# One level of Strassen's method in the second product of a channel mixing: seven block products in place of eight

## The chip, the cores and the metric

The kernel runs on one core of a Trainium2 chip. The metric is the device time of one execution in microseconds (us). The median of three runs is compared before and after the change.

## What is computed

Attention with a window of 64 over 4 sequences of 576 tokens, then a gated block that mixes along the tokens, then a token mixing, and last the channel mixing, which is what the change touches. Tokens of all sequences together: 2304. Width 512, hidden width of the channel mixing 1536.

```python
def _moe2_ref(x, w_tok1, w_tok2, w_ch1, w_ch2):
    xt = x.transpose(0, 2, 1)
    h = np.maximum(xt @ w_tok1, 0.0) @ w_tok2
    u = x + h.transpose(0, 2, 1)
    h2 = np.maximum(u @ w_ch1, 0.0) @ w_ch2     # u: 2304 x 512, w_ch1: 512 x 1536, w_ch2: 1536 x 512
    return (u + h2).astype(np.float32)
```

The weights come as 64-bit floats.

## The kernel before

Every operand of a matrix product is a pair of two fp32r tiles, a rounded part h and a rest l, and a product is three matmuls: h·h, h·l, l·h (`mm3`, L128). So a tile that is to be multiplied is first copied by ScalarE into h, and VectorE subtracts to get l. A weight is read from HBM as 64-bit words into `wraw`, and `load_wide` (L110) makes it fp32: one `Abs` on ScalarE (L123), four integer steps on VectorE (`to_f32`, L56 to L62), then the cast to h on ScalarE (L125) and the subtraction to l on VectorE (L126).

The activations stay in SBUF as `U`, 128 partitions x 4 x 2304. Up to L513 the order of every engine is written out by hand (attention and the gated block). Behind that the order is a planner's: it simulates the program and lets each engine take, among the instructions that are ready in its simulation, the one that comes first in the program. The order it finds is then fixed, and each engine works through its queue in that order on the chip. A pool that is opened where another one was closed gets its memory; its tiles wait for the last readers and writers of what lay there.

The stages behind L513, as the program has them:

- `wout(c)` (L544): output product of the gated block, five chunks of 512 tokens (the last one 256).
- `x2nat(b)` (L563), `tok1(b)` (L573), `tok2(b)` (L586): the token mixing of sequence b. 20 transposes, 28 matmuls of 512 columns, 48 matmuls of 288 columns. VectorE adds the result of `tok2` to `U` (L594).
- Loads of the channel weights between these: `load_c1(pl, ft)` for the 12 column blocks of `w_ch1`, `load_c2(pl, k)` for the 12 row blocks of `w_ch2`. All 24 blocks stay in SBUF as h and l.
- The channel mixing (L689 to L707): chunks of 512 tokens, four full ones and one of 256. `uin(c)` (L635) splits the chunk of `U`. `ch1(u, ft)` (L645) makes one of 12 hidden tiles: 12 matmuls into a bank of `psmm`, a ReLU on ScalarE to `g3h` (L653) and the rest `g3l` on VectorE (L654). `ch2` (L657) adds its product to the four output banks `acc`: 12 matmuls (L664). The planner has `uin(0)` and three `ch1` of the first chunk (L666, L670, L679) at hand while the token mixing still runs. Behind each chunk VectorE adds `acc` to `U` (L706) and SP stores it (L707).

Names that the steps below use: `psmm` 3 banks, `psA` 5 banks, `nat` (splits of the token mixing), `hp` (hidden tiles of the token mixing), `lw` (work space of the loads). All DMAs are issued by SP in order.

## Time and profile before

| | us |
|---|---|
| median of 3 runs | 674.54 |
| runs | 674.00 to 675.59 |
| profiled execution, span from the first to the last instruction | 675.1 |
| TensorE busy in it | 646.6 (96%) |
| VectorE busy | 358.1 (53%) |
| ScalarE busy | 247.1 (37%) |
| GpSimd busy | 21.7 (3%) |

The profiled execution has no time of its own beside its span; the span stands for it, 0.6 us above the median of the runs. A busy TensorE in this profile means that a matmul is in flight; matmuls overlap, so how dense they run is read from the distance between their starts.

### The profile page before, as it was taken

To read this page: it belongs to the slowest core of one execution; us is meant where nothing else is said; L and a number is where in the kernel's file an instruction comes from. 1 tells how busy PE (TensorE), PEld (TensorE's weight loads), DVE (VectorE), ACT (ScalarE), POOL (GpSimd) and SP (SyncE) were. 2 spreads that over 40 slices of the span, in tenths; PEclk is the share of its full clock that TensorE was granted. 3 is DMA by queue.
4 is the path that set the end of the run, shared out by engine and by line. 5 is a ranking of instruction groups with operands and counts; after the bars stand their busy time and mean duration, and the time that the engine had idled before them with its cause. 6 is when DMAs were issued, how large, how long until landed. Compare 5 with 4: busy or idle time off the path is not lost.

```text
span 675.1 us, 10865 instructions
## 1 busy us (share of the span) xinstructions
PE 646.6 (96%) x4346; PEld 551.8 (82%) x4346; DVE 358.1 (53%) x900; ACT 247.1 (37%) x654; POOL 21.7 (3%) x49
## 2 busy tenths in 40 slices
...
GB/s 319 234 121 88 143 164 149 96 105 84 71 145 29 3 108 130 65 1 0 11 146 94 94 124 157 0 63 0 1 1 62 1 0 22 42 1 1 62 1 32
DMA packets 27954, 50.18 MB, mean 74 GB/s; under 512 B 2432, under 2 KB 12544, under 8 KB 27904
## 3 DMA queue, kind: packets, MB, share of 16 engines
...
q8 instruction: 34, 0.56, 0.4%
...
## 4 chain that ended last, share of the span: by engine, by line
PE 84%; DVE 7%; ACT 5%; DMA 3%; issue 1%; SPq 0%; POOL 0%; DVEq 0%; ACTq 0%
PE mm L136 51%; PE A L664 22%; PE A L136 4%; ACT pb L234 3%; PE sc L212 1%; PE xo L263 1%; PE A L570 1%; DVE pb L243 1%; ACT PT L252 1%; DMA raw<-in_wsT 1%; PE pt L251 1%; DMA msk<-in_mask 1%; DVE val L61 1%; DVE val L62 1%; PE mm L159 1%
## 5 line engine op out<-in xcount | busy, mean ns | idle before, releaser
L654 DVE SCALAR_TENSOR_TENSOR g3l<-mm,g3h 128x512 fp32r<-128x512 f32 (+1 forms) x60 | 38.2, 637 | 180.8 <-ACT g3h L653 180.6
L653 ACT ACTIVATE g3h<-mm 128x512 fp32r<-128x512 f32 (+1 forms) x60 | 33.4, 556 | 216.6 <-PE mm L136 216.5
L136 PE MATMUL mm<-uh,c1l 128*128 128x512 f32 (+1 forms) x240 | 89.0, 371 | 0.0
L136 PE MATMUL mm<-uh,c1h 128*128 128x512 f32 (+1 forms) x240 | 89.0, 371 | 0.0
L136 PE MATMUL mm<-ul,c1h 128*128 128x512 f32 (+1 forms) x240 | 88.9, 370 | 0.0
L664 PE MATMUL A<-g3h,c2l 128*128 128x512 f32 (+1 forms) x240 | 88.6, 371 | 0.0
L664 PE MATMUL A<-g3h,c2h 128*128 128x512 f32 (+1 forms) x240 | 87.5, 372 | 0.0
L664 PE MATMUL A<-g3l,c2h 128*128 128x512 f32 (+1 forms) x240 | 84.2, 372 | 0.0
L136 PEld LDWEIGHTS mm<-ul,c1h 128*128 128x128 f32 x240 | 45.2, 188 | 8.2
L664 PEld LDWEIGHTS A<-g3h,c2h 128*128 128x128 f32 x240 | 45.2, 188 | 8.2
L136 PEld LDWEIGHTS mm<-uh,c1h 128*128 128x128 f32 x240 | 45.3, 189 | 8.1
L136 PEld LDWEIGHTS mm<-uh,c1l 128*128 128x128 f32 x240 | 45.2, 188 | 8.2
L664 PEld LDWEIGHTS A<-g3h,c2l 128*128 128x128 f32 x240 | 45.2, 188 | 8.1
L664 PEld LDWEIGHTS A<-g3l,c2h 128*128 128x128 f32 x240 | 44.3, 188 | 8.3
L136 PE MATMUL mm<-ws_h,nh 128*128 128x288 f32 x160 | 47.5, 301 | 0.9 <-DVE tmp L354 0.9
L136 PE MATMUL mm<-ws_l,nh 128*128 128x288 f32 x160 | 46.5, 295 | 0.0
L234 ACT ACTIVATE pb<-pb,nm 128x128 f32<-128x128 f32 x96 | 37.2, 396 | 2.6 <-DVE nm L229 2.5
L136 PE MATMUL mm<-ws_h,nl 128*128 128x288 f32 x128 | 37.8, 295 | 0.0
L136 PE MATMUL mm<-xh,wi_h 128*128 128x384 f32 x96 | 32.6, 340 | 0.0
L136 PE MATMUL mm<-xh,wi_l 128*128 128x384 f32 x96 | 32.1, 334 | 0.0
L136 PE MATMUL mm<-xl,wi_h 128*128 128x384 f32 x96 | 32.1, 334 | 0.0
L136 PE MATMUL mm<-wi_h,xl 128*128 128x512 f32 x72 | 29.6, 411 | 2.1 <-DVE xl L272 2.0
...
## 6 DMA issues: line engine op xcount, KB each, us to landing
wraw<-in_w_c SPq DMA_DIRECT2D x24, 512.0 KB, 3.5
...
qq<-in_qT SPq DMA_DIRECT2D x18, 256.0 KB, 4.3
va<-in_v SPq DMA_DIRECT2D x18, 256.0 KB, 2.8
vb<-in_v SPq DMA_DIRECT2D x18, 256.0 KB, 3.3
U<-in_w_in SPq DMA_DIRECT2D x8, 512.0 KB, 6.9
outT<-U SPq DMA_DIRECT2D x16, 256.0 KB, 2.3
raw<-in_w_out SPq DMA_DIRECT2D x8, 256.0 KB, 2.9
```

The lines of the kernel that those rows point to most:

```text
L61: nc.vector.scalar_tensor_tensor(out=xi, in0=high, scalar=-0x40000000, in1=xi, op0=ALU.bitwise_and, op1=ALU.bitwise_or)
L62: nc.vector.scalar_tensor_tensor(out=xi, in0=low, scalar=29, in1=xi, op0=ALU.logical_shift_right, op1=ALU.bitwise_or)
L136: nc.tensor.matmul(o, a, c, start=(i == 0), stop=(i == n - 1))
L159: nc.tensor.matmul(ps.rearrange("p (a c) -> p a c", a=4), ident16, ident16.unsqueeze(1).to_broadcast([P, 4, 128]), start=True, stop=True)
L212: nc.tensor.matmul(scs[e][64 * q:64 * q + 64, j, :], qq[er, j, 64 * q:64 * q + 64], kk[er, j, step * q:step * q + 128], start=not on_pe, s ...
L234: nc.scalar.activation(out=pb[:, h, :], in_=scs[g][:, h - 4 * g, :] if mk is None else pb[:, h, :], func=AF.Exp, scale=SCALE, bias=nm[:, h ...
L243: nc.vector.tensor_tensor(out=half, in0=half, in1=rs.unsqueeze(2).to_broadcast([P, 4, 128]), op=ALU.mult)
L251: nc.tensor.transpose(pt[:, h, :], pb[:, 4 * g + h, :], ident)
L252: nc.scalar.copy(out=PT[:, 4 * g:4 * g + 4, :], in_=pt)
L653: nc.scalar.activation(out=gh, in_=ps, func=AF.Relu)
L654: nc.vector.scalar_tensor_tensor(out=gl, in0=ps, scalar=0.0, in1=f(gh), op0=ALU.max, op1=ALU.subtract)
L664: nc.tensor.matmul(acc[d], a, c, start=(ft == 0 and i == 0), stop=(ft == 11 and i == 2))
```

## The change

The second product of the channel mixing, `w_ch2`^T times the hidden activations, is cut in two by two blocks: the hidden width in halves of 768 (six tiles, `NJ` = 6), the output width in halves of 256, the tokens of a chunk in halves of 384 (`HW`). Seven block products take the place of eight, each of 6 x 2 x 3 matmuls of 384 columns. A chunk is now 768 tokens (`TW`), three chunks in all.

- `load_c2(j)` now makes, of rows j and j + 6 of `w_ch2`, the eight 256-column blocks that the method wants (four of them sums and differences by GpSimd), splits seven into h and l and writes them to a scratch tensor `scr` in HBM. Six calls: 0 to 2 during the token mixing, 3 to 5 in the first chunk.
- `ch1` makes 384-column halves and writes the ReLU as plain fp32 tiles `H` (30 buffers), by ScalarE alone. GpSimd makes the differences `e` and `b12` as the tiles come, and later, in place, those of `b11` and `b21` (`diff`).
- `product` reads the weights of a block product from `scr`, 512 KB at a time (`w`, 7 buffers), splits each hidden block into `oh` and `ol` (4 buffers each) by a ScalarE copy and a VectorE subtraction, and issues its 36 matmuls. `p1`, `u2`, `u3` hold partial results; VectorE (`vec`) and GpSimd add them to `U`, SP stores.
- The loads are in another order, `tok1(1)` now stands behind the closing of the pools of `wout`, and `uin(0)` stands behind the whole token mixing: its pool `up` opens where the work space of the loads (`lw3`, `xw`) was closed.

```diff
@@ -577,8 +577,8 @@
             ps = psA.tile([P, 512], F32, tag="A", name="A")
             mm3(ps, [(t1_h[:, s, jc], t1_l[:, s, jc], xn[b][s][0], xn[b][s][1]) for s in range(4)],
                 [(t1_h[:, 4, jc], xn[b][4]), (t1_l[:, 4, jc], xn[b][4])])
-            hh = hp.tile([P, 512], F32R, tag="hh", name="hh", bufs=2)
-            hl = hp.tile([P, 512], F32R, tag="hl", name="hl", bufs=2)
+            hh = hp.tile([P, 512], F32R, tag="hh", name="hh", bufs=hbufs)
+            hl = hp.tile([P, 512], F32R, tag="hl", name="hl", bufs=hbufs)
             nc.scalar.activation(out=hh, in_=ps, func=AF.Relu)
             nc.vector.scalar_tensor_tensor(out=hl, in0=ps, scalar=0.0, in1=f(hh), op0=ALU.max, op1=ALU.subtract)
             ht[b].append((hh, hl))
@@ -593,8 +593,11 @@
                 mm3(ps[:, :288], [(ht[b][j][0][:, dc], ht[b][j][1][:, dc], t2_h[:, j, cs], t2_l[:, j, cs]) for j in range(2)])
                 nc.vector.tensor_tensor(out=us, in0=ps[:, :288], in1=us, op=ALU.add)
 
-    c_stack = ExitStack()
-    c1, c2 = {}, {}
+    c_stack, x_stack = ExitStack(), ExitStack()
+    c1 = {}
+    hbufs = 2
+    HW, TW, NJ = 384, 768, 6
+    scr = tc.dram_tile([8, NJ // 2, P, 2, 2, 256], F32, name="scr")
 
     def load_c1(pl, ft):
 
@@ -602,110 +605,205 @@
         load_wide(lw, *[t.rearrange("p k c -> p (k c)") for t in c1[ft]],
                   w_c1[:, 128 * ft:128 * ft + 128].rearrange("(k p) c -> p k c", p=P), wmax=wmax)
 
-    def load_c2(pl, k):
-        c2[k] = [pl.tile([P, DM], F32R, name=f"c2{x}{k}") for x in "hl"]
-        load_wide(lw, *c2[k], w_c2[128 * k:128 * k + 128, :], wmax=wmax)
+    def fetch(dst, src):
+
+        raw = lw.tile([P, 2 * wmax], F32, tag="wraw", name="wraw", bufs=3).bitcast(I32)[:, :2 * DM]
+        nc.sync.dma_start(out=raw, in_=src.bitcast(I32))
+        r3 = raw.rearrange("p (n w) -> p n w", w=2)
+        nc.scalar.activation(out=dst, in_=f(r3[:, :, 1]), func=AF.Abs)
+        to_f32(dst, r3[:, :, 0], r3[:, :, 1])
+
+    def load_c2(j):
+
+        X = xw.tile([P, 8, 256], F32, tag="X", name="X", bufs=1)
+        for r, s in ((j, 0), (j + NJ, 2)):
+            fetch(X[:, s:s + 2, :].rearrange("p a c -> p (a c)"), w_c2[128 * r:128 * r + 128, :])
+        for o, a, b, op in ((4, 1, 3, ALU.add), (5, 4, 0, ALU.subtract), (6, 0, 1, ALU.subtract), (7, 2, 5, ALU.subtract)):
+            nc.gpsimd.tensor_tensor(out=X[:, o, :], in0=X[:, a, :], in1=X[:, b, :], op=op)
+        for s, n in ((0, 1), (2, 2), (4, 2), (6, 2)):
+            hl = xw.tile([P, 2, 2, 256], F32R, tag="hl", name="hl", bufs=3)[:, :n]
+            nc.scalar.copy(out=hl[:, :, 0, :], in_=X[:, s:s + n, :])
+            nc.vector.tensor_tensor(out=hl[:, :, 1, :], in0=X[:, s:s + n, :], in1=f(hl[:, :, 0, :]), op=ALU.subtract)
+            nc.sync.dma_start(out=scr[s:s + n, j // 2, :, j % 2].rearrange("s p h c -> p s h c"), in_=f(hl))
+
+    def xpool(stack, **kw):
+        return pool(f"xw{len(c1)}", stack=stack, bufs=1, **kw)
 
     wout(0)
     run_work(len(work))
     ws_stack.close()
     c1p = pool("c1p", "left", stack=c_stack, bufs=1)
-    hp = pool("hp", "left", stack=c_stack, bufs=1)
+    xw = xpool(x_stack, side="left")
+    hp = pool("hp", "left", stack=x_stack, bufs=1)
     wout(1)
     x2nat(0)
+    load_c1(c1p, 0)
     wout(2)
     tok1(0)
-    load_c1(c1p, 0)
+    load_c2(0)
     x2nat(1)
+    load_c1(c1p, 6)
     wout(3)
     tok2(0)
+    load_c2(1)
     load_c1(c1p, 1)
-    tok1(1)
     wout(4)
     x2nat(2)
-    load_c1(c1p, 2)
-    load_c1(c1p, 3)
+    load_c1(c1p, 7)
+    x_stack.close()
     g_stack.close()
 
 
-    p3 = pool("p3", "left", stack=c_stack, bufs=1)
+    c1q = pool("c1q", "left", stack=c_stack, bufs=1)
     wmax = DM
-    lw = pool("lw3", "left", stack=c_stack, bufs=1)
-
...
-    u0 = uin(0)
+    hbufs = 4
+    hp = pool("hp2", "right", stack=t_stack, bufs=1)
+    lw = pool("lw3", "left", stack=x_stack, bufs=1)
+    xw = xpool(x_stack, side="left")
+    tok1(1)
+    load_c2(2)
     tok2(1)
     tok1(2)
     x2nat(3)
-    g0 = [ch1(u0, ft) for ft in range(2)]
+    load_c1(c1q, 2)
+    load_c1(c1q, 8)
+    tok1(3)
     tok2(2)
-    load_c1(p3, 4)
-    load_c2(p3, 0)
-    tok1(3)
-    load_c1(p3, 5)
-    load_c2(p3, 1)
-    load_c2(p3, 2)
-    load_c1(p3, 6)
-    g0.append(ch1(u0, 2))
+    load_c1(c1q, 3)
+    load_c1(c1q, 9)
     tok2(3)
+    x_stack.close()
     t_stack.close()
     r_stack.close()
-    c2p = pool("c2p", "right", bufs=1)
-    load_c2(c2p, 3)
-    for k in range(4, 12):
-        load_c2(c2p, k)
-        if k < 9:
-            load_c1(c2p, k + 3)
-    chunks = range(-(-NTOK // CW))
-    for c in chunks:
-        u = uin(c) if c else u0
-        w = u[0].shape[-1]
-        acc = [psA.tile([P, 512], F32, tag="A", name="A")[:, :w] for _ in range(4)]
-        gq = [] if c else g0
-
-        late = 9 if c == chunks[-1] else 12
-        for ft in range(12):
-            while len(gq) < min(ft + 2, 12):
-                gq.append(ch1(u, len(gq)))
-            if ft < late:
-                ch2(acc, gq[ft], ft)
-        for d in range(4):
-            for ft in range(late, 12):
-                ch2(acc, gq[ft], ft, (d,))
-            ts_ = slice(CW * c, CW * c + w)
-            nc.vector.tensor_tensor(out=U[:, d, ts_], in0=acc[d], in1=U[:, d, ts_], op=ALU.add)
-            nc.sync.dma_start(out=outT[128 * d:128 * d + 128, ts_], in_=U[:, d, ts_])
+
+    up = pool("up", "left", stack=c_stack, bufs=1)
+    op_ = pool("op", "left", stack=c_stack, bufs=1)
+    Hp = pool("Hp", "right", stack=c_stack, bufs=1)
+    lw = pool("lw4", "left", stack=x_stack, bufs=1)
+    xw = xpool(x_stack, side="left")
+
+    def uin(c):
+        uh = up.tile([P, 4, TW], F32R, tag="uh", name="uh")
+        ul = up.tile([P, 4, TW], F32R, tag="ul", name="ul")
+        for h in range(2):
+            hs = slice(HW * h, HW * h + HW)
+            us = U[:, :, TW * c + HW * h:TW * c + HW * h + HW]
+            nc.scalar.copy(out=uh[:, :, hs], in_=us)
+            nc.vector.tensor_tensor(out=ul[:, :, hs], in0=us, in1=f(uh[:, :, hs]), op=ALU.subtract)
+        return uh, ul
+
+    def ch1(u, ft):
+
+        uh, ul = u
+        out = []
+        for h in range(2):
+            hs = slice(HW * h, HW * h + HW)
+            ps = psmm.tile([P, 512], F32, tag="mm", name="mm")[:, :HW]
+            mm3(ps, [(c1[ft][0][:, k, :], c1[ft][1][:, k, :], uh[:, k, hs], ul[:, k, hs]) for k in range(4)])
+            t = Hp.tile([P, HW], F32, tag="H", name="H", bufs=30)
+            nc.scalar.activation(out=t, in_=ps, func=AF.Relu)
+            out.append(t)
+        return out
+
+    def diff(out, a, b):
+        nc.gpsimd.tensor_tensor(out=out, in0=a, in1=b, op=ALU.subtract)
+        return out
+
+    def product(acc, slot, blk, first, last):
+
+        for jj in range(NJ // 2):
+            w = wr.tile([P, 2, 2, 256], F32R, tag="w", name="w", bufs=7)
+            nc.sync.dma_start(out=f(w), in_=scr[slot, jj])
+            for j in (2 * jj, 2 * jj + 1):
+                oh = op_.tile([P, HW], F32R, tag="oh", name="oh", bufs=4)
+                ol = op_.tile([P, HW], F32R, tag="ol", name="ol", bufs=4)
+                nc.scalar.copy(out=oh, in_=blk[j])
+                nc.vector.tensor_tensor(out=ol, in0=blk[j], in1=f(oh), op=ALU.subtract)
+                for d in range(2):
+                    dc = slice(128 * d, 128 * d + 128)
+                    todo = [(w[:, j % 2, 0, dc], oh), (w[:, j % 2, 1, dc], oh), (w[:, j % 2, 0, dc], ol)]
+                    for i, (a, m) in enumerate(todo):
+                        nc.tensor.matmul(acc[d], a, m, start=(first and j == 0 and i == 0),
+                                         stop=(last and j == NJ - 1 and i == 2), skip_group_check=True)
+
+    def banks():
+        return [psA.tile([P, 512], F32, tag="A", name="A")[:, :HW] for _ in range(2)]
+
+    u = None
+    for c in range(NTOK // TW):
+        t0 = TW * c
+        u = uin(c)
+        b11, b12, b21, b22, e = [], [], [], [], []
+        for j in range(NJ):
+            if c == 0 and j + 1 < NJ:
+                for ft in (j + 1, j + 1 + NJ):
+                    if ft not in c1:
+                        load_c1(c1q, ft)
+                if j < 3:
+                    load_c2(3 + j)
+            x, y = ch1(u, j)
+            b11.append(x)
+            b12.append(y)
+            x, y = ch1(u, j + NJ)
+            b21.append(x)
+            b22.append(y)
+            e.append(diff(Hp.tile([P, HW], F32, tag="H", name="H", bufs=30), b12[j], b11[j]))
+            diff(b12[j], b22[j], b12[j])
+        if c == 0:
+            x_stack.close()
+            wr = pool("wr", "left", stack=c_stack, bufs=1)
+        us = [[U[:, 2 * dh:2 * dh + 2, t0 + HW * h:t0 + HW * h + HW] for h in range(2)] for dh in range(2)]
+
+        def vec(dst, src, add, d, eng=nc.vector):
+            eng.tensor_tensor(out=dst, in0=src, in1=add, op=ALU.add)
+
+        def store(dh, h, d):
+            r = slice(256 * dh + 128 * d, 256 * dh + 128 * d + 128)
+            nc.sync.dma_start(out=outT[r, t0 + HW * h:t0 + HW * h + HW], in_=us[dh][h][:, d, :])
+
+        def tmp(tag):
+            return [wr.tile([P, HW], F32, tag=f"{tag}{d}", name=tag) for d in range(2)]
+
+        A = banks()
+        product(A, 0, b11, True, True)
+        p1 = tmp("p1")
+        for d in range(2):
+            nc.scalar.copy(out=p1[d], in_=A[d])
+            vec(us[1][0][:, d, :], us[1][0][:, d, :], p1[d], d, nc.gpsimd)
+        for j in range(NJ):
+            diff(b11[j], b22[j], e[j])
+        Bk = banks()
+        product(Bk, 5, b11, True, True)
+        u2 = tmp("u2")
+        for d in range(2):
+            vec(u2[d], Bk[d], p1[d], d)
+            vec(us[0][1][:, d, :], us[0][1][:, d, :], u2[d], d, nc.gpsimd)
+        product(A, 2, b21, False, True)
+        for d in range(2):
+            vec(us[0][0][:, d, :], A[d], us[0][0][:, d, :], d)
+            store(0, 0, d)
+        for j in range(NJ):
+            diff(b21[j], b21[j], b11[j])
+        product(Bk, 6, b12, False, True)
+        u3 = tmp("u3")
+        for d in range(2):
+            vec(u3[d], Bk[d], p1[d], d)
+            vec(us[1][1][:, d, :], us[1][1][:, d, :], u3[d], d, nc.gpsimd)
+        C = banks()
+        product(C, 4, e, True, True)
+        for d in range(2):
+            vec(us[1][1][:, d, :], C[d], us[1][1][:, d, :], d)
+            store(1, 1, d)
+        product(Bk, 3, b21, False, True)
+        for d in range(2):
+            vec(us[1][0][:, d, :], Bk[d], us[1][0][:, d, :], d)
+            store(1, 0, d)
+        product(C, 7, b22, False, True)
+        for d in range(2):
+            vec(us[0][1][:, d, :], C[d], us[0][1][:, d, :], d)
+            store(0, 1, d)
     c_stack.close()
+
 
 
 def kernel(**inputs):
```

## Rows read from the trace of the kernel before

**Rows 1.** The page: busy time by engine, transfer rate in 40 slices, chain by engine.

```profile
PE 646.6 (96%) x4346; PEld 551.8 (82%) x4346; DVE 358.1 (53%) x900; ACT 247.1 (37%) x654; POOL 21.7 (3%) x49
...
GB/s 319 234 121 88 143 164 149 96 105 84 71 145 29 3 108 130 65 1 0 11 146 94 94 124 157 0 63 0 1 1 62 1 0 22 42 1 1 62 1 32
...
PE 84%; DVE 7%; ACT 5%; DMA 3%; issue 1%; SPq 0%; POOL 0%; DVEq 0%; ACTq 0%
```

**Rows 2.** Busy time by stretch: us, then each engine (instructions), granted clock, DMA.

```profile
289.00:336.00 47.00, 47.00 (x268) 41.26 (x268) 15.77 (x29) 16.02 (x32) 0.00 (x0) 1.00 0.00 1
336.00:388.00 52.00, 52.00 (x303) 46.37 (x302) 42.75 (x79) 20.85 (x33) 0.00 (x0) 1.00 0.33 112
```

**Rows 3.** Chain of waits in order of time: start, us, what (x matmuls).

```profile
506.47 5.47 PE mm L136 x24
511.94 2.72 PE A L664 x12
...
525.99 2.80 PE A L664 x12
...
572.98 5.47 PE mm L136 x24
...
654.39 1.41 PE A L664 x12
```

**Rows 4.** Timeline of TensorE: start, us of one, line, tiles, shapes.

```profile
202.63 0.34 PE L136 MATMUL mm<-xl,wi_h 128*128 128x384 f32 x1
...
210.60 0.33 PE L136 MATMUL mm<-xh,wi_l 128*128 128x384 f32 x1
...
362.52 0.39 PE L664 MATMUL A<-g3h,c2h 128*128 128x512 f32 x1
...
364.01 0.39 PE L136 MATMUL A<-nl,t_h 128*128 128x512 f32 x1
```

**Rows 5.** Groups by line and shape: busy us, mean ns | idle before, releaser.

```profile
L61 DVE SCALAR_TENSOR_TENSOR wval<-wraw,wval 128x512 int32<-128x512 int32 x26 | 17.6, 684 | 0.1
...
L594 DVE TENSOR_TENSOR U<-mm,U 128x288 f32<-128x288 f32 x32 | 14.4, 454 | 22.0 <-PE mm L136 21.9
...
L58 DVE TENSOR_SCALAR wval<-wval 128x512 f32<-128x512 f32 x26 | 10.9, 422 | 3.0 <-ACT wval L123 2.5
...
L553 DVE TENSOR_TENSOR gl<-U,gh 128x512 fp32r<-128x512 f32 x16 | 10.4, 684 | 2.0 <-ACT gh L552 2.0
...
L552 ACT CAST gh<-U 128x512 fp32r<-128x512 f32 x16 | 9.2, 631 | 0.4 <-PE mm L136 0.3
...
L642 DVE TENSOR_TENSOR ul<-U,uh 128x2048 fp32r<-128x2048 f32 x4 | 9.1, 2286 | 2.2 <-ACT uh L641 2.2
...
L405 POOL TENSOR_TENSOR wi_l<-val,wi_h 128x512 fp32r<-128x512 f32 x4 | 5.1, 1280 | 9.1 <-ACT wi_h L403 9.1
...
L553 DVE TENSOR_TENSOR gl<-U,gh 128x256 fp32r<-128x256 f32 x4 | 1.7, 426 | 4.9 <-ACT gh L552 4.9
...
L552 ACT CAST gh<-U 128x256 fp32r<-128x256 f32 x4 | 1.6, 407 | 0.6 <-PE mm L136 0.5
```

**Rows 6.** Timeline of VectorE and GpSimd at two places in the hand-written part.

```profile
36.66 0.69 DVE L243 TENSOR_TENSOR pb<-pb,rs 128x512 f32<-128x512 f32 x1
37.33 1.27 POOL L405 TENSOR_TENSOR wi_l<-val,wi_h 128x512 fp32r<-128x512 f32 x1 [6.59 <-ACT wi_h L403]
37.67 1.48 DVE L243 TENSOR_TENSOR pb<-pb,rs 128x512 f32<-128x512 f32 x1
...
53.14 0.69 DVE L223 TENSOR_REDUCE mx<-sc 128x4 f32<-128x512 f32 x1
53.16 1.27 POOL L405 TENSOR_TENSOR wi_l<-val,wi_h 128x512 fp32r<-128x512 f32 x1 [2.46 <-ACT wi_h L403]
```

**Rows 7.** The page's DMA issues: engine, count, KB each, median us from issue to landing.

```profile
wraw<-in_w_c SPq DMA_DIRECT2D x24, 512.0 KB, 3.5
...
outT<-U SPq DMA_DIRECT2D x16, 256.0 KB, 2.3
```

38 lines of the change are left out of this document (7 added, 31 removed).

## The prediction

> **What bounds the kernel now.** I read the page first: TensorE is busy 96% of the span and makes 84% of the chain that ended last; VectorE is at 53%, GpSimd at 3% [rows 1]. A busy share says nothing of how dense the matmuls run, so the second view is the chain in order of time. From 506.47 to 572.98 it is TensorE alone: 24 matmuls of `ch1`, then 12 of `ch2` and 12 of `ch1` in turn, no wait between them [rows 3]. One such chunk is 12 x (12 + 12) = 288 matmuls, so its 66.51 us are 0.2309 us a matmul of 512 columns. Third, the stretches: TensorE has no idle time from 289 to 388 either, its granted clock is 1.00 (the 2.4 GHz level), while VectorE is busy 15.8 of 47 us in the first of them and 42.8 of 52 in the second [rows 2]. So the end is set by the number and the distance of matmuls, and VectorE is the engine next in line before 388. Fourth, the order: a `ch2` matmul at 362.52 stands between matmuls of `tok1` (the next one shown is at 364.01) [rows 4], though the program has them in separate calls. The queues are interleaved by the planner, and `ch1` and `ch2` of the first chunk fill holes of the token mixing.
>
> **The matmuls.** Before: four chunks of 66.51 us, and a last one with 256 columns, 12 matmuls of which take 1.41 us [rows 3], so 288 take 33.8 us. Together 299.9 us. After: a chunk has 24 halves of `ch1` with 12 matmuls (288) and 7 products with 36 (252); three chunks have 1620, all of 384 columns. The gated block has such matmuls: between the starts at 202.63 and 210.60 lie 46 steps [rows 4], 0.1733 us each. 1620 x 0.1733 = 280.7 us, a gain of 19.2 us. What may spoil it: `ch2` of 512 columns shows two speeds in one chunk, 2.72 and 2.80 us for 12 [rows 3], at the same clock, 6.7 ns a matmul apart. The rows of 384 show only one speed, so I take 0.1733; if all 1620 paid the 6.7 ns, 10.9 us of the gain would go. That is the other bound.
>
> The rows put 13 ns on a matmul of 384 columns beyond its 384 / 2.4 = 160 ns. The Trainium skill ("TensorE: Matmul & The Clock Gate", Back-to-back issue gap) has N / 2.4 + 2.5 ns; by that 1620 x 162.5 ns = 263.3 us against 1152 x 215.8 + 288 x 109.2 ns = 280.0 us, an estimate of 16.8 us gain. This case's rows are longer at every width, and the rows decide.
>
> **The splits, beside TensorE.** `ch1` loses the 60 subtractions of L654; each hidden block of a product costs a cast and a subtraction of 384 columns. The cast lies between 407 and 631 ns, the subtraction between 426 and 684 [rows 5]: 0.52 and 0.56 us. TensorE takes 6 x 0.1733 = 1.04 us for that block, so alone they are hidden; 126 of each add 65 us of ScalarE and 70 of VectorE to engines that were nearly idle there.
>
> **GpSimd beside VectorE.** A difference of 512 columns took GpSimd 1280 ns [rows 5]; 384 columns are 0.96 us. Per chunk 12 fall into `ch1` and 18 (12 differences, 6 additions to `U`) into the products. The trace shows what that does to VectorE: a two-input operation on SBUF (L243) takes 0.69 us alone; the one that started at 37.67, while GpSimd's subtraction ran from 37.33 to 38.60, took 1.48 and ended 0.55 us after GpSimd did. A reduction from PSUM (L223) beside GpSimd's next one kept its 0.69 [rows 6]. So `ol` (two SBUF inputs) and the differences exclude each other; VectorE's additions from PSUM don't. In the products of a chunk: 42 x 0.56 = 23.5 us of `ol`, 18 x 0.96 = 17.3 us of GpSimd, 3.4 us of the next `uin` (two of 0.75 x 2.286 us [rows 5]): 44.2 us against 42 x 1.04 = 43.7 us of matmuls. That just fits on average, but GpSimd's work is bunched. The differences of `b21` come ready one per block; a block then needs 0.56 + 0.96 = 1.52 us for TensorE's 1.04, 0.48 us lost per step. Four buffers of `ol` are three steps ahead, 3.1 us, less 1.1 us for cast and subtraction: 2.0 us of cover. Ten GpSimd operations in a row (two additions, six differences, two additions) cost 4.8 - 2.0 = 2.8 us. Below: 0, where the planner puts `ch1` of the next chunk into the hole, as it did at 362.52. Above: 5 us, two such rows without cover. One more wait is new there: on GpSimd the program puts two additions, which wait for the end of the first product and its copy `p1`, ahead of the differences of `b11`. Kept in that order, the second product starts late by a cast (0.52), three operations (2.9) and its first split (1.1), 4.5 us a chunk, which is within the upper bound. I take 2 us a chunk, 6 us in all, nearer to the lower end, since the planner is seen to fill holes; bounds 0 and 15.
>
> This is also where a page speaks against the change: the Trainium skill ("SBUF — State Buffer", SBUF: two separate sides) makes the port pair of VectorE and GpSimd an exclusive lock for a whole instruction. The trace agrees (1.48 us in place of 0.69).
>
> **The weights by way of HBM.** A product reads 3 x 512 KB per 6.24 us. Seven buffers are 7 x 2.08 = 14.6 us ahead; such a transfer lands 3.5 us after its issue [rows 7]. With seven loaded during `ch1`, the other 14 are 7.3 MB in 43.7 us, 168 GB/s; the first slice of the page moved 319 GB/s for 17 us [rows 1]. Hidden, 0 us. Without that cover see the second rival. Making the blocks costs VectorE, by call of `load_c2`: two conversions of 2 x 0.422 + 2 x 0.684 = 2.21 us, and splits of 0.43 + 3 x 0.684 = 2.48: 6.9 us, a `load_c1` 2.21 + 0.68 = 2.9 us [rows 5].
>
> **Up to 336.** Two `load_c2` go here, 13.8 us; VectorE has 31 us free from 289 to 336 [rows 2]. 0 us, at most 2.
>
> **End of the token mixing.** Behind 336 the changed program has three `tok1` (28 x 0.2267 = 6.35 us each), three `tok2` (48 of 288 columns; scaled from 0.1733, 6.35) and one `x2nat`: about 40 us of TensorE, and none of the `ch1` and `ch2` that filled it. VectorE has six ReLU rests (0.684), 24 additions (0.454), ten splits (0.68), one `load_c2` and four `load_c1`: 4.1 + 10.9 + 6.8 + 6.9 + 11.6 = 40.3 us in the same 40 us. And then `uin(0)`, whose memory comes free only behind the last of these loads: 1.7 us for its first half on VectorE, and about as much on ScalarE. Bounds: 0, if the loads run ahead; 9 us, if VectorE is only as dense as from 336 to 388, 42.75 of 52 [rows 2] (40.3 / 0.82 = 49). I take 4.
>
> **First chunk.** Until its sixth pair of `ch1`, 5 x 48 x 0.1733 = 41.6 us, three `load_c2` and four `load_c1` have to be through: 32.3 us of VectorE; GpSimd has 12 differences of 0.64 and ten of 0.96, 17.3 us. If all excluded each other, the last weights were 8 us late; if none, on time. I take 2: VectorE kept up at 42.75 of 52 without TensorE waiting [rows 2]. Later chunks need no loads, and their `uin` runs during products.
>
> **End.** The last block's store is of 192 KB, less than the 256 KB that land in 2.3 us [rows 7], more than the 128 KB of before: 0.2 us, at most 0.5.
>
> **Sum.** 675.1 - 19.2 + 6 + 4 + 2 + 0.2 = 668.1 us of span. The runs' median lies 0.6 us under this span, so 667.5 us. With all terms at the lower ends 655.5; its own range is 659 to 675.
>
> **Rivals.** (1) GpSimd locks VectorE out, slower. If every pair excludes and GpSimd's queue has the next operation ready each time, VectorE gets no turn within a bunch. From the start of the products to the end of the fourth, 24 `ol` (13.4), 17 to 18 GpSimd operations (17) and `uin` (3.4) need 34 us for 25 us of matmuls, less 2 of cover: 7 us a chunk, 21 in all; with 8 us in the first chunk and 4 before it 33 us: 688; half of it 678. It decides from 19.2 us of loss on. For: rows 6 and the sum of 44.2 against 43.7. Against: of the 18 operations only the six differences of `b11` have a reader in the next product, and they may begin before `ch1` is through. By the lock on the page named above it would come to the same time.
> (2) Weights behind stores, slower. SP works in order; a store waits for the end of a product and its addition. If weight loads are queued behind each of the four pairs of stores, a product begins 3.5 + 0.5 us late, four times a chunk, 48 us: 715. Against: 14.6 us of lead, and a planner that orders SP too.
> (3) The slow matmul speed at 384 columns: 667.5 + 10.9 = 678. Against: rows 4.
> (4) All holes filled: 655.5 to 659.
>
> **How the numbers follow.** Forecast 0.69, rival 1 0.14, rival 2 0.04, rival 3 0.05, rival 4 0.08. The range 657 to 680 leaves out half of rival 4, a good half of rival 1 and rival 2, some 0.17. A measurement of this kernel can tell about 0.2% (1.35 us) from no change: faster is under 673.2, slower over 675.9. Faster: 0.66 + 0.08 + 0.03 from the lower ends of rivals 1 and 3 = 0.77; same 0.04; slower 0.19.
>
> **What would show it.** Right: 384-column matmuls 0.173 us apart in `ch1` and in `product`; chunks of about 93.6 us (540 matmuls) plus 1 to 4; `ol` of 0.56 us alone and about 1.5 beside GpSimd; a hole of some us in TensorE before the first `ch1`; no wait for `w`. Wrong: a step of 0.18 us; TensorE waiting on `ol` in each product (rival 1), or on the DMA of `w` with a store in front of it on SP (rival 2); a hole before `ch1` well over 9 us, as the loads would then be the bound.

## The result and the profile after

| us | before | after |
|---|---|---|
| median of 4 runs each, measured together | 674.27 (673.01 to 675.59) | 668.79 (667.56 to 670.31) |
| ratio, 95% interval | | 0.9914 (0.9888 to 0.9940) |
| span of the profiled execution | 675.1 | 665.8 |

The change makes the kernel 5.5 us faster; 667.5 was forecast, 657 to 680 as the range. The profiled execution after is one of 667.56 us, 1.8 us above its span.

The page of after: busy time by engine, the groups of the new splits and differences, the transfers of the weights (columns as in [rows 1, 5, 7]).

```profile
PE 629.4 (95%) x4526; PEld 582.0 (87%) x4526; DVE 440.6 (66%) x995; ACT 317.1 (48%) x811; POOL 149.1 (22%) x163
...
L721 DVE TENSOR_TENSOR ol<-H,oh 128x384 fp32r<-128x384 f32 x126 | 95.4, 783 | 88.5 <-ACT oh L720 80.6
...
L709 POOL TENSOR_TENSOR H<-H 128x384 f32<-128x384 f32 x72 | 82.6, 1157 | 120.5 <-ACT H L704 80.3
...
w<-scr SPq DMA_DIRECT2D x63, 512.0 KB, 4.3
```

TensorE is 17 us less busy, VectorE 82 us more, GpSimd 127 us more [rows 1]. Where time went is read by stage. The first and last starts of some of TensorE's matmuls cut the end of the kernel in three: from the first matmul of `wout` to the first of `ch1` (token mixing), from there to the first of a product (first chunk), and from there to the end. First of before:

```profile
L136 PE MATMUL mm<-gh,wo_h x80: 280/389/487, 261.3 to 335.1; 128*128 128x512 f32 x64, 128*128 128x256 f32 x16
...
L664 PE MATMUL A<-g3l,c2h x240: 279/393/399, 363.8 to 671.1; 128*128 128x512 f32 x96, 128*128 128x256 f32 x24
```

Then of after (count, ns least/median/most, first and last start in us):

```profile
L136 PE MATMUL mm<-gh,wo_h x80: 278/389/485, 257.7 to 334.2; 128*128 128x512 f32 x64, 128*128 128x256 f32 x16
...
L136 PE MATMUL mm<-uh,c1h x288: 334/334/689, 369.4 to 617.3; 128*128 128x384 f32 x144
...
L726 PE MATMUL A<-oh,w x504: 334/334/346, 430.7 to 661.2; 128*128 128x384 f32 x168
...
L726 PE MATMUL A<-ol,w x252: 333/334/441, 431.0 to 661.5; 128*128 128x384 f32 x126
```

From the first matmul of `wout` to the last of all it is 671.1 - 261.3 = 409.8 us before and 661.5 - 257.7 = 403.8 after: 6.0 us less, which agrees with the medians. (`wout` begins 3.6 us earlier, in the part that the change doesn't touch; the kernels below begin it between 256.8 and 261.7. So stages are compared, not places.) The stretches of after, by engine:

```profile
369.40:430.70 61.30, 54.41 (x290) 51.99 (x290) 43.68 (x61) 26.96 (x53) 29.72 (x27) 0.94 0.58 203
430.70:524.40 93.70, 93.70 (x542) 93.70 (x541) 41.13 (x56) 36.22 (x70) 33.42 (x30) 1.00 0.47 157
524.40:618.00 93.60, 93.60 (x542) 93.60 (x541) 41.13 (x56) 36.23 (x70) 33.42 (x30) 1.00 0.42 135
618.00:662.00 44.00, 43.87 (x253) 43.36 (x251) 32.79 (x49) 20.70 (x41) 17.75 (x15) 1.00 0.60 195
```

Columns: stretch, us, then PE, PEld, DVE, ACT, POOL with instructions, granted clock, DMA share, GB/s. From the first product on TensorE has no hole: 540 matmuls in 93.6 us are 0.1733 us each. The loss is in the first line: 288 matmuls, 49.9 us at that pace, take 61.3. So the bill is 19.2 us gained on matmuls, 11.4 lost in the first chunk, and the remaining 1.8 lost in the token mixing (111.7 us, where before has 109.9: its 409.8 less the 299.9 of matmuls in its channel mixing).

What TensorE does in that hole, from its timeline (a group that waited has its wait in brackets):

```profile
410.79 0.34 PE L136 MATMUL mm<-uh,c1l 128*128 128x384 f32 x1
415.21 0.69 PE L136 MATMUL mm<-uh,c1h 128*128 128x384 f32 x1 [4.09 <-ACT c1h L125]
415.70 0.53 PE L136 MATMUL mm<-ul,c1h 128*128 128x384 f32 x1
...
421.13 0.33 PE L136 MATMUL mm<-uh,c1l 128*128 128x384 f32 x1
```

The stretch behind the longest wait, with the granted clock (0.51) as the third number from the end:

```profile
415.21:421.10 5.89, 5.84 (x17) 5.34 (x18) 5.86 (x10) 2.13 (x5) 1.39 (x2) 0.51 0.48 179
```

What TensorE waited for from 369 to 431 (us in total, times, longest):

```profile
PE mm L136 <- ACT c1h L125: 4.1, 1, 4.1
PE mm L136 <- ACT H L704: 1.8, 2, 1.4
PE mm L136 <- DVE c1l L126: 1.0, 1, 1.0
```

The larger part is for blocks of `w_ch1`, the rest for ScalarE's ReLU. By the starts, five waits between 394 and 417 are 7.9 us. Behind the longest one, 4.2 us by the starts, the matmuls stand 0.32 us apart and not 0.1733: the granted clock is at its lower level (1.2 GHz) from 415.21 to 421.1, 17 matmuls in 5.9 us for 2.9. One of the five waits, 0.4 us, lies in that stretch, so the clock costs some 2.6 us; the rest of the 11.4 is smaller delays.

Why the block is late, first from what SyncE's queue waited for (369 to 432):

```profile
SPq L611 <- PE mm L136: 10.2, 1, 10.2
```

and its issues in order:

```profile
369.55 7.21 SPq L611 DMA_DIRECT2D wraw<-in_w_c  x4
...
393.88 0.38 SPq L118 DMA_DIRECT2D wraw<-in_w_c  x1
```

The reads of the last three `load_c2` (L611) waited 10.2 us for a matmul of `tok2(3)` and began as it ended: the work space `lw4` and `xw` lies where the hidden tiles of the token mixing (`hp2`) lay. The first of the last four `load_c1` (L118) is issued 24 us later, behind all six of those reads. And then VectorE, by group and shape, with GpSimd behind it, in this stretch:

```profile
L626 DVE TENSOR_TENSOR hl<-X,hl 128x512 fp32r<-128x512 f32 x9 | 9.2, 1018 | 4.8 <-ACT hl L625 4.6
L61 DVE SCALAR_TENSOR_TENSOR X<-wraw,X 128x512 int32<-128x512 int32 x6 | 5.3, 892 | 0.1
L60 DVE TENSOR_SCALAR X<-X 128x512 int32<-128x512 int32 x6 | 4.2, 693 | 0.1
L62 DVE SCALAR_TENSOR_TENSOR X<-wraw,X 128x512 int32<-128x512 int32 x6 | 4.0, 681 | 0.0
...
L709 POOL TENSOR_TENSOR H<-H 128x384 f32<-128x384 f32 x15 | 19.2, 1291 | 14.6 <-ACT H L704 14.6
L622 POOL TENSOR_TENSOR X<-X 128x256 f32<-128x256 f32 x12 | 10.8, 907 | 38.1 <-DVE X L62 37.8
```

The split of 512 columns takes 1.02 us here for 0.68 in [rows 5], the shift of L60 0.69 for 0.42. So two causes offer themselves: loads that start late, and conversions that GpSimd makes longer. The experiments test them.

### The profile page after: what moved, and what is told of

It reads as the page before. It is cut to its first block, busy times and chain, and to the rows that moved or that the text cites. A ratio compares the mean times of both kernels' runs of the same rounds, so it can differ in the third digit from the quotient of the medians.

```text
span 665.8 us, 12069 instructions
## 1 busy us (share of the span) xinstructions
PE 629.4 (95%) x4526; PEld 582.0 (87%) x4526; DVE 440.6 (66%) x995; ACT 317.1 (48%) x811; POOL 149.1 (22%) x163
## 4 chain that ended last, share of the span: by engine, by line
PE 43%; DVE 3%; DMA 2%; POOL 1%; issue 1%; ACT 1%; DVEq 0%; POOLq 0%; ACTq 0%; SPq 0%
PE mm L136 21%; PE A L726 20%; PE A L136 2%; DMA wraw<-in_w_c 2%; POOL H L709 1%; DVE X L58 0%; DVE hl L626 0%; POOL X L622 0%; DVE X L61 0%; DVE wval L62 0%; DVE wval L61 0%; PE A L570 0%; DVE nl L295 0%; DVE wval L60 0%; DVE X L62 0%
## 5 line engine op out<-in xcount | busy, mean ns | idle before, releaser
L721 DVE TENSOR_TENSOR ol<-H,oh 128x384 fp32r<-128x384 f32 x126 | 95.4, 783 | 88.5 <-ACT oh L720 80.6
L726 PE MATMUL A<-oh,w 128*128 128x384 f32 x504 | 113.8, 334 | 0.0
L709 POOL TENSOR_TENSOR H<-H 128x384 f32<-128x384 f32 x72 | 82.6, 1157 | 120.5 <-ACT H L704 80.3
L136 PE MATMUL mm<-uh,c1h 128*128 128x384 f32 x288 | 97.4, 341 | 5.9 <-ACT c1h L125 4.1
L136 PE MATMUL mm<-uh,c1l 128*128 128x384 f32 x288 | 96.8, 338 | 1.0 <-DVE c1l L126 1.0
L136 PE MATMUL mm<-ul,c1h 128*128 128x384 f32 x288 | 96.9, 338 | 0.0
L720 ACT CAST oh<-H 128x384 fp32r<-128x384 f32 x126 | 64.2, 515 | 67.1 <-PE A L726 51.9
L726 PEld LDWEIGHTS A<-oh,w 128*128 128x128 f32 x504 | 89.7, 188 | 0.0
L726 PE MATMUL A<-ol,w 128*128 128x384 f32 x252 | 69.8, 334 | 0.0
L726 PEld LDWEIGHTS A<-ol,w 128*128 128x128 f32 x252 | 45.9, 188 | 0.2 <-DVE ol L721 0.2
L252 ACT COPY PT<-pt 128x512 f32<-128x512 f32 x36 | 19.7, 592 | 30.4 <-PE pt L251 30.4
```

The costliest lines, as they stand in the source:

```text
L136: nc.tensor.matmul(o, a, c, start=(i == 0), stop=(i == n - 1))
L252: nc.scalar.copy(out=PT[:, 4 * g:4 * g + 4, :], in_=pt)
L709: nc.gpsimd.tensor_tensor(out=out, in0=a, in1=b, op=ALU.subtract)
L720: nc.scalar.copy(out=oh, in_=blk[j])
L721: nc.vector.tensor_tensor(out=ol, in0=blk[j], in1=f(oh), op=ALU.subtract)
L726: nc.tensor.matmul(acc[d], a, m, start=(first and j == 0 and i == 0), stop=(last and j == NJ - 1 and i == 2), skip_group_check=True)
```

## The experiments

All medians are of 4 runs unless said; the kernel before ran beside them (medians 674.7 to 675.0). The stages are read as above, from first starts, and the last one ends with the last `oh` matmul. Each is read from one execution. After, e4 and e6 have the same program up to the products and differ there by 1.9 us (172.6 to 174.5), so smaller differences between sums of stages say little:

| kernel | median us | token mixing | first chunk | products | first two together |
|---|---|---|---|---|---|
| after | 668.79 | 111.7 | 61.3 | 230.5 | 173.0 |
| e1_c1_first | 668.75 | 111.7 | 60.3 | 233.2 | 172.0 |
| e2_no_sums | 662.63 | 111.9 | 56.2 | 230.5 | 168.1 |
| e3_room | 663.54 | 113.6 | 54.5 | 230.5 | 168.1 |
| e7_both | 664.62 | 115.9 | 51.8 | 230.5 | 167.7 |
| e8_vec_sums | 666.05 | 111.0 | 59.4 | 230.5 | 170.4 |
| e9_x2 | 665.27 | 113.8 | 55.4 | 230.6 | 169.2 |
| e12_c1f_vec_x2 | 665.15 | 118.9 | 49.9 | 230.5 | 168.8 |
| e13_room3_x | 660.69 | 113.9 | 50.9 | 230.5 | 164.8 |
| e14_order | 663.19 | 116.7 | 49.9 | 230.5 | 166.6 |
| e4_eight | 688.73 | 112.4 | 62.1 | 249.3 | 174.5 |
| e5_twice (10 runs) | 675.30 | 111.9 | 65.1 | 233.8 | 177.0 |
| e6_w2 | 689.49 | 111.4 | 61.2 | 249.5 | 172.6 |

**The hole: is it the order of the loads?** e1_c1_first puts the last four `load_c1` ahead.

```diff
-            if c == 0 and j + 1 < NJ:
-                for ft in (j + 1, j + 1 + NJ):
-                    if ft not in c1:
-                        load_c1(c1q, ft)
-                if j < 3:
-                    load_c2(3 + j)
+            if c == 0 and j < 3:
+                if j < 2:
+                    load_c1(c1q, 4 + j)
+                    load_c1(c1q, 10 + j)
+                load_c2(3 + j)
```

> The changed kernel lost about 11 us in TensorE between 390 and 431, in the first chunk. Here only the order of the loads in that chunk is changed: the four load_c1 come ahead of the second and third load_c2. Theory A, the order is at fault (the column blocks of w_ch1 stand behind three load_c2 in the queues): no TensorE wait for c1h or c1l any more, the hole goes and the time falls by 8 to 11 us against the changed kernel (668.8), to about 658 to 661. Theory B, the whole of the conversions starts too late (the memory of lw4 and xw is free only when the token mixing has ended, at 369.5) and takes some 50 us whatever the order: the hole moves from ch1 to the front of the first product, which waits for the first w; the time stays within 2 us of 668.8.

Measured 668.75, ratio to before 0.9916 (0.9887 to 0.9945): no change. What TensorE waited for from 368 to 429 in this kernel:

```profile
PE mm L136 <- ACT H L704: 3.8, 4, 2.7
PE A L726 <- DMA w<-scr: 3.2, 1, 3.2
```

No wait for a block of `w_ch1` is left; now the first product waits for its weights, which are read back only when the last `load_c2` is through, and 2.7 us more go in the products. The order alone only moves the hole.

**Is it where the loads start?** e3_room opens the pool of `oh` and `ol` behind the loads, so their work space moves down by 12 KB a partition, and halves the buffers of `hp2`, so that the raw reads don't lie on it any more and `xw` less.

```diff
-    hbufs = 4
+    hbufs = 2
-    op_ = pool("op", "left", stack=c_stack, bufs=1)
...
         if c == 0:
             x_stack.close()
+            op_ = pool("op", "left", stack=c_stack, bufs=1)
```

> Pools alone: op (oh and ol) is opened together with wr behind the loads, and hp2 has 2 buffers in place of 4, so that lw4 and the front of the last xw lie beside hp2 and not on it. The loads of the first chunk can then start when the work space of the loads before is free, about 352, not at 369.5. Theory B: the 11 us hole goes nearly whole, 657 to 661; the first product starts its splits only behind the loads, which may cost up to 2 us. Theory A: the order is as before, so ch1 still waits for its c1, by less: 662 to 666. Theory C: the conversions are as slow as before but earlier, so the same as theory B; only e2 tells these two apart.

Measured 663.54, ratio 0.9836 (0.9794 to 0.9878), 5.3 us better than after, less than this theory wanted.

```profile
L136 PE MATMUL mm<-uh,c1h x288: 334/334/522, 374.4 to 615.6; 128*128 128x384 f32 x144
...
L725 PE MATMUL A<-oh,w x504: 334/334/346, 428.9 to 659.4; 128*128 128x384 f32 x168
```

The first chunk takes 54.5 us instead of 61.3; the token mixing pays 1.9 of it back. Only the raw reads came earlier: the first conversion of the fourth `load_c2` still started at 374.6, as `X` kept waiting for the end of `tok2(3)`. The median lies in the range of theory A, but TensorE waits for no block of `w_ch1` in this chunk. Its one wait is for a ReLU, and the ReLU stood in ScalarE's queue behind the `Abs` of a `load_c1` (L123) whose read had not landed:

```profile
407.40 0.67 ACT L123 ACTIVATE wval<-wraw 128x512 f32<-128x512 f32 x1 [2.39 <-DMA wraw<-in_w_c]
407.98 0.47 ACT L703 ACTIVATE H<-mm 128x384 f32<-128x384 f32 x1
...
408.50 0.44 PE L136 MATMUL mm<-uh,c1h 128*128 128x384 f32 x1 [2.51 <-ACT H L703]
```

So a queue that loads and ReLUs share is a third thing that can hold TensorE up; no run tests it alone. e7_both adds e1's order to e3:

> The edits of e1 and e3 together. Theory B: as e3 or 1 to 2 us better, 656 to 660. Theory A: the order is what counts, so as e1. If the hole is gone, the rest of the sum holds: TensorE without a wait from 257 to the end, about 657 us.

Measured 664.62, ratio 0.9844 (0.9804 to 0.9884), above the 656 to 660 of theory B and not told apart from e3. The first chunk is down to 51.8, but the four `load_c1` now run on VectorE beside the token mixing, which takes 115.9.

**Is it GpSimd in VectorE's way?** e2_no_sums leaves the four sums of GpSimd out of the last three `load_c2`; other blocks are split and stored in their place, so only the sums are missing.

```diff
-        for o, a, b, op in ((4, 1, 3, ALU.add), ...):
+        for o, a, b, op in () if j > 2 else ((4, 1, 3, ALU.add), ...):
...
+            r = s % 4 if j > 2 else s
-            nc.scalar.copy(out=hl[:, :, 0, :], in_=X[:, s:s + n, :])
+            nc.scalar.copy(out=hl[:, :, 0, :], in_=X[:, r:r + n, :])
```

> The four sums on GpSimd are left out of the last three load_c2 (the unsummed blocks are split and stored in their place, so these weights are other numbers); the rest is the changed kernel. Theory C, GpSimd keeps VectorE out of its port during the conversions: VectorE's operations in the first chunk fall back to their lone durations but for the differences of H, and the hole of 11 us shrinks by 4 to 8 us, to about 661 to 665. Theory B (late start): the chain of a load_c2 loses only the time of the sums that are not hidden, the hole shrinks by 0 to 3 us, to about 666 to 669.

Measured 662.63, ratio 0.9817 (0.9787 to 0.9846): 6.2 us for twelve operations of 0.9 us. But this has two readings: VectorE's steps get shorter, or the chain within one `load_c2` (conversion, four sums, splits, then the next block in the same `X`) does. e8_vec_sums and e9_x2 try to tell them apart. In e8 VectorE makes those sums:

```diff
-            nc.gpsimd.tensor_tensor(out=X[:, o, :], ...
+            (nc.vector if j > 2 else nc.gpsimd).tensor_tensor(out=X[:, o, :], ...
```

> Nothing is left out: in the last three load_c2 the four sums of 256 columns are made by VectorE in place of GpSimd. Leaving them out gave 662.6. Theory C, VectorE is short of time in the first chunk, and GpSimd's exclusion makes its steps longer: the exclusion goes, but 12 x 0.43 = 5.2 us of VectorE come, so 666 to 669. Theory D, the chain of one load_c2 through its single X (conversion, four GpSimd steps of 1 us, splits, then the next block) is what is long: each chain gets 4 - 1.7 = 2.3 us shorter, three of them 6.9 us, so about as without the sums, 662 to 664.

Measured 666.05, ratio 0.9882 (0.9848 to 0.9915), in the range that theory C, VectorE's time, gave. One sum on VectorE (its row: count, ns least/median/most, starts):

```profile
L622 DVE TENSOR_TENSOR X<-X x12: 411/414/1122, 376.1 to 408.8; 128x256 f32<-128x256 f32 x12
```

The first chunk of e2, then of e8:

```profile
370.10:426.30 56.20, 52.91 (x290) 52.59 (x289) 39.92 (x61) 26.69 (x53) 19.98 (x15) 0.94 0.64 222
...
368.10:427.50 59.40, 54.03 (x291) 52.27 (x290) 44.90 (x73) 27.17 (x53) 18.92 (x15) 0.94 0.60 209
```

And what VectorE waited for in a `load_c2`, ScalarE's copy `hl`, in the first chunk of after, then of e8:

```profile
DVE hl L626 <- ACT hl L625: 4.9, 6, 2.3
...
DVE hl L626 <- ACT hl L625: 0.3, 1, 0.3
```

Without the sums VectorE is 3.8 us less busy than in after (39.92 for 43.68). In e8 it is 1.2 us busier than in after, and yet the chunk is 1.9 us shorter, as it waits 4.6 us less. So the time follows theory C, but the steps from engine to engine within a `load_c2` have a part in the 6.2 us; the two parts are not separated.

e9 is e3 with a second buffer for `X`, so that two blocks can be under way:

```diff
-        X = xw.tile([P, 8, 256], F32, tag="X", name="X", bufs=1)
+        X = xw.tile([P, 8, 256], F32, tag="X", name="X", bufs=2 if j > 2 else 1)
```

> As e3_room (pool op opened behind the loads, hidden tiles of the token mixing in two buffers), and X with two buffers in the last three load_c2, so that a block's conversion need not wait for the splits of the block before. Theory D (chain through the single X): 3 to 5 us under e3_room's 663.5, so 658 to 661. Theory C (VectorE is short of time, lengthened by GpSimd): as e3_room, 662 to 665.

Measured 665.27, ratio 0.9862 (0.9833 to 0.9890): no better than e3, and 0.3 above the range of theory C. So the single `X` by itself isn't what holds. VectorE waits 0.4 us for `hl` in the first chunk, where e3 has 4.1, but is busy 43.5 us for 40.2, and GpSimd 32.7 for 30.4: the wait has turned into longer operations, which fits two engines that exclude each other.

**Both causes together.** e12_c1f_vec_x2 is e7 with VectorE's sums and the second `X`:

> Nothing left out: e7_both (room, and the last four load_c1 ahead), with the sums of the last three load_c2 by VectorE and two buffers of X. If the first chunk is bound by VectorE's and GpSimd's time alone, the gains add: 664.6 - 2.7 = 662, and what remains is in the token mixing, which e7 slowed by 4.5 us between 360 and 370. If the chain through X was what held up the rest, 659 or less.

Measured 665.15, ratio 0.9856 (0.9830 to 0.9882); 662 was expected. The first chunk has no hole at all (49.9), but the token mixing takes 118.9. TensorE's longest wait there is for additions of `tok2` (L594). They stood in VectorE's queue behind steps of a `load_c1` (L58 to L61), and those behind an `Abs` on ScalarE that had waited 2.8 us for its read:

```profile
370.91 0.43 DVE L58 TENSOR_SCALAR wval<-wval 128x512 f32<-128x512 f32 x1 [1.72 <-ACT wval L123]
...
372.44 1.18 DVE L594 TENSOR_TENSOR U<-mm,U 128x288 f32<-128x288 f32 x3
...
372.95 0.40 PE L136 MATMUL mm<-t_h,hh 128*128 128x288 f32 x1 [2.44 <-DVE U L594]
```

It is e3's picture again, a load that is free to run early but not yet there when its turn in a fixed queue comes. e13_room3_x keeps the order of after, gives `hp2` three buffers and `X` a pool of its own just beside it, and has the sums on VectorE:

```diff
-    hbufs = 4
+    hbufs = 3
-    op_ = pool("op", "left", stack=c_stack, bufs=1)
     lw = pool("lw4", "left", stack=x_stack, bufs=1)
+    xx = pool("xx", "left", stack=x_stack, bufs=1)
     xw = xpool(x_stack, side="left")
...
-        X = xw.tile([P, 8, 256], F32, tag="X", name="X", bufs=1)
+        X = (xx if j > 2 else xw).tile([P, 8, 256], F32, tag="X", name="X", bufs=1)
```

(and e8's line, and `op_` opened as in e3)

> Nothing left out: op opened behind the loads, three buffers of hidden tiles in the token mixing, X in a pool of its own that lies beside the memory of hp2, and the sums of the last three load_c2 by VectorE. So the fourth load_c2 can be converted before the last matmul of tok2(3), which e3 could not (its X waited until 374.5). Theory (memory that holds back the loads, and VectorE's time, are what make the hole): 1.1 us of conversion and more come earlier, the hole shrinks from e3's 5 us to 1 to 3, 658 to 661. If VectorE's time alone counts: 663.5 - 2.7 = 661.

Measured 660.69 (659.37 to 663.68), ratio 0.9800 (0.9768 to 0.9833): 8.1 us better than after, 14 better than before and the lowest median of all. It fits both expectations. Its stretches before and in the first chunk:

```profile
340.00:375.40 35.40, 34.57 (x219) 31.37 (x219) 33.47 (x65) 13.97 (x22) 3.90 (x4) 1.00 0.36 127
375.40:426.30 50.90, 50.51 (x291) 49.87 (x290) 36.18 (x61) 25.21 (x51) 21.48 (x15) 1.00 0.64 233
```

Two of VectorE's groups from the first of these stretches, where GpSimd has little to do:

```profile
L61 DVE SCALAR_TENSOR_TENSOR X<-wraw,X 128x512 int32<-128x512 int32 x4 | 2.6, 682 | 0.0
...
L60 DVE TENSOR_SCALAR X<-X 128x512 int32<-128x512 int32 x4 | 1.6, 416 | 0.0
```

They are back at 0.68 and 0.42 us, from the 0.89 and 0.69 of the first chunk of after. Two of the four are of the fourth `load_c2`, which is now converted before the first `ch1`, as the theory wanted. VectorE is busy 33.5 of 35.4 us at the end of the token mixing, the clock stays at 1.00, and the first chunk is 1 us from dense. In the first two stages e3 saved 4.9 us, e8 2.6, and e13, which has both edits and more room for `X`, 8.2: near the sum. e12, which has both too, saved 4.2, so that the two add is shown for one arrangement only. e14_order only moves the four `load_c1` of e13 between the three `load_c2`:

```diff
-            if c == 0 and j + 1 < NJ:
-                for ft in (j + 1, j + 1 + NJ):
-                    if ft not in c1:
-                        load_c1(c1q, ft)
-                if j < 3:
-                    load_c2(3 + j)
+            if c == 0 and j < 3:
+                load_c2(3 + j)
+                if j < 2:
+                    load_c1(c1q, 4 + j)
+                    load_c1(c1q, 10 + j)
```

> As e13_room3_x, with the last four load_c1 put between the last three load_c2 in the program (c2, two c1, c2, two c1, c2). If the hole in ch1 is only moved to the front of the first product, as e1_c1_first did: within 1 us of e13. If the order counts once there is room: 2 us less.

Measured 663.19, ratio 0.9834 (0.9809 to 0.9860). Neither expectation holds: it is not better, by the medians 2.5 us worse, though the intervals overlap. By the stages 1.0 us is gained in the first chunk and 2.8 are lost in the token mixing, where TensorE's waits for L594 rise from 0.7 to 3.1 us.

**Do matmuls alone set the end behind the first chunk?** e4_eight issues the last product twice.

```diff
-        product(C, 7, b22, False, True)
+        product(C, 7, b22, False, False)
+        product(C, 7, b22, False, True)
```

> The seventh block product (with b22) is issued a second time, so there are eight, and C gets that product twice: its values are not the method's. Step tested: once the products run, TensorE's matmuls alone set the end, 0.1733 us each. If so, 3 chunks x 36 matmuls x 0.1733 = 18.7 us more than the changed kernel's 668.8: 687.5. If the engines beside TensorE set it (rival: the conversions of blocks, 6 x (0.56 of VectorE and 0.52 of ScalarE) a product, or the reads of weights), the extra product would be hidden in part (under 684) or cost its conversions on top (over 690).

Measured 688.73, ratio 1.0202 (1.0170 to 1.0235). The products stage:

```profile
L726 PE MATMUL A<-oh,w x576: 334/334/346, 433.4 to 682.7; 128*128 128x384 f32 x192
```

249.3 us for 230.5: 18.8 more, where 18.7 of matmuls was expected. The eighth block product that the method saves is worth its matmuls and nothing else, in all three chunks.

**How far is rival 1?** e5_twice makes the differences of `b11` and `b21` twice.

```diff
             diff(b11[j], b22[j], e[j])
+            diff(b11[j], b22[j], b11[j])
...
             diff(b21[j], b21[j], b11[j])
+            diff(b21[j], b21[j], b11[j])
```

> The twelve GpSimd differences of b11 and b21, which lie among the products, are made twice, so 36 more GpSimd operations of about 1.16 us; b11 and b21 then hold other values than the method's. Theory (the products have slack because ch1 of the next chunk is put among them, and VectorE and GpSimd fit side by side with 41.1 and 33.4 of 93.7 us busy): 33.4 + 13.9 = 47.3 us of GpSimd and 41.1 of VectorE still fit in 93.7, so 0 to 2 us more than 668.8. Rival 1 of the prediction (GpSimd locks VectorE out, and the margin is small): each extra 1.16 us delays a conversion that TensorE waits for, 0.5 to 1.16 us each, 18 to 42 us more: 687 to 711.

Measured 675.30, 6.5 us more than after: more than the theory's 2, far from the rival's 18. By stretch, from the first `ch1` on:

```profile
370.30:435.40 65.10, 56.14 (x290) 53.48 (x289) 45.12 (x61) 27.14 (x53) 34.14 (x31) 0.92 0.54 192
435.40:529.00 93.60, 93.60 (x541) 93.47 (x541) 46.14 (x56) 36.19 (x70) 46.91 (x42) 1.00 0.46 156
529.00:622.60 93.60, 93.60 (x541) 93.41 (x540) 46.20 (x56) 36.20 (x70) 46.96 (x42) 1.00 0.41 136
622.60:669.50 46.90, 45.88 (x254) 43.39 (x253) 38.54 (x48) 20.70 (x41) 28.19 (x23) 1.00 0.55 183
```

In the two stretches in which `ch1` of the next chunk is put among the products, 13.5 us more of GpSimd cost nothing. The last products have no `ch1` beside them, and there the exclusion reaches TensorE: 3.3 us (230.5 to 233.8), and it waits for `ol`, where all the products of after have one such wait of 0.2 us:

```profile
PEld A L726 <- DVE ol L721: 3.4, 8, 1.3
```

The rest is in the first chunk, 3.8 us more (e4 and e6, which change nothing there, have 62.1 and 61.2): GpSimd has four more operations there, beside the conversions. That these are the cause is argued, not shown.

**What does the lead of the weights hide?** e6_w2 gives `w` two buffers in place of seven (`bufs=7` to `bufs=2`).

> Weights w with two buffers in place of seven. The step tested: the reads from HBM cost nothing because they run 14.6 us ahead. With two buffers a read is issued when the matmuls of the buffer before are through, one use of 2.08 us ahead, and lands 4.3 us later: two blocks of weights take 2.08 + 4.3 us for 4.16 of matmuls, 1.1 us lost at each. In the first two chunks ch1 of the next chunk (50 us) can fill that; in the last one nothing can: 21 x 1.1 = 23 us, 692 in all. If a lone transfer lands in 2.9 us as the store of hl does, 21 x 0.41 = 8.6 us, 677. If the lead isn't needed: 669. If SP's order (rival 2: weights behind stores) counts without the lead, the losses sit at the four pairs of stores, 4 us each, also in the first two chunks, over 700.

Measured 689.49, ratio 1.0221 (1.0199 to 1.0243).

```profile
434.30:528.00 93.70, 93.70 (x541) 93.37 (x540) 39.41 (x56) 36.21 (x70) 32.33 (x30) 1.00 0.41 135
528.00:621.60 93.60, 93.33 (x537) 92.65 (x536) 38.27 (x56) 36.11 (x70) 32.27 (x30) 1.00 0.41 136
621.60:684.00 62.40, 49.24 (x259) 43.72 (x257) 29.07 (x49) 20.75 (x41) 17.36 (x15) 1.00 0.54 179
```

Nearly the whole loss of 19.0 us is in the last stretch, which takes 62.4 us to the last start for the 43.5 of after (618.0 to 661.5); the first two are as fast with two buffers as with seven. What TensorE waited for there:

```profile
PE A L726 <- DMA w<-scr: 12.7, 18, 1.6
```

These are 12.7 us; the rest stands with TensorE's weight loads and is put down to `oh` or to nothing. A transfer landed in 3.3 us (median), and the loss lies between the two prices that were expected. Stores in front of weights on SP, rival 2, would also have shown in the first two chunks: they did not.

## Why the prediction was right, step by step

The time is 1.3 us from the forecast, but its terms are not: one of 6 us was nothing, one of 4 was 1.8, one of 2 was 11.4. The losses were forecast as 12.2 us and came to some 13; that they are so close is luck, as the errors cancel.

**The matmuls** (19.2 us gained): right. 540 in 93.6 us are the 0.1733 us of [rows 4], and e4 gives the same price for 108 more. Rival 3, the slower pitch, didn't come.

**The splits**: hidden, as said. `oh` took 0.515 us against 0.52 worked out. `ol` took 0.78 in the mean for the 0.56 of one alone.

**GpSimd beside VectorE, in the products** (6 us): the mechanism is there, in the 0.78, and costs nothing. The step that failed is the sum of 44.2 us against 43.7: it set the work of the products against the products alone, while `ch1` lies among them, as the text itself says of 362.52, and the stretch for it is 93.6 us. The lower bound was right. Only the last chunk has just the 44 us; there 10.4 us more of GpSimd (28.19 for 17.75) cost 3.3 in e5. So rival 1 was near in the last chunk alone.

**The weights by way of HBM** (0): right; by e6 the cover is worth 19 us, nearly all of it in the last chunk, since in the others `ch1` would hide the reads too.

**End of the token mixing** (4 us): nearly the lower bound. It came to 1.8 us. The step that failed is that `uin(0)`, waiting for the last loads, would hold `ch1` up. It did wait, 2.4 us for a store of `hl`, but that wait ended at 351.9 with its first cast, 17 us before the first `ch1`, which followed `tok2(3)` without a hole.

**First chunk** (2 us, bounds 0 to 8): measured 11.4, above the upper bound. The step counted VectorE's 32.3 us against 41.6 of matmuls, and said that VectorE kept up at 42.75 of 52 before [rows 2]. GpSimd's 17.3 us were 29.7: 15 differences of 1.29 us and twelve sums of 0.91, for ten of 0.96 and twelve of 0.64. Three things were missing: that these loads can't start before the last `tok2` is through, since their memory is under it (e3: 4.9 us with a part of it); that the stretch of before had no GpSimd in it, so its density was no measure (e8: 2.6 us, e2: 4.9, by longer operations of VectorE and by steps from engine to engine); and that the waits let the clock fall (2.6 us of the 11.4 by the timeline; e13, which has hardly a wait, keeps 1.00). A fourth, a step that TensorE needs standing in a queue behind a load whose read has not landed, is seen in traces alone (e3: 2.5 us; e12, in the token mixing: 2.4). The first was to be read from the program: the prediction asked where the memory of `uin(0)` lay, but not where that of the loads did.

**From span to time** (-0.6): harmless, but not understood. The forecast amounts to the median of before less 7.0 us; by the stages it was 6.0, by the medians 5.5. Wherever a time and a span are known of one execution, the time is 1.7 to 2.2 us above the span, not 0.6 below, so before's 675.1 belongs to an execution slower than the runs shown. The forecast span, 668.1, is 2.3 us above the 665.8 measured.

**End** (0.2 us): right. From the last matmul's start to the end of the span it is 4.0 us before and 4.3 after.

The Trainium skill ("SBUF — State Buffer", SBUF: two separate sides) has the lock between VectorE and GpSimd also for VectorE's operations in a two-port mode, not only for those with two inputs. For the products the prediction counted the latter alone. The trace agrees as far as L60, with one input, went from 0.42 to 0.69 us; whether it runs in that mode no run shows.

What stays open: how the gain of e2 divides between VectorE's longer operations and the chain of a `load_c2`; and why e12 loses 7 us in the token mixing where e13 loses 2. The wait for L594 and the lower clock behind it are a part of that (the granted clock is 0.91 from 360 to 378.6 in e12 and 1.00 in e13), the rest isn't traced. A version with the sums on VectorE in all six `load_c2` wasn't run.
